# A fused SSM-convolution and gated-MLP kernel with its gradients: tables built earlier, four step buffers, spectral sets at named places, and the last phase's loads moved

## The chip, the cores and the metric

The kernel runs on one core of one Trainium2 chip. The metric is device microseconds of one execution; before the change the median of three runs is 498.83 us (498.76 to 499.54). All times in the views of the profile are microseconds from the start of one profiled execution unless they are marked ns. PE is TensorE's matmul stream, PEld its weight loads, DVE VectorE, ACT ScalarE, POOL GpSimd, SP the queue from which nearly all DMAs are issued.

## The reference

With S = 2048 rows, D = 512 and F = 1376, everything in bf16:

```python
xn = layernorm(x)                         # x = A_q, no weights
k_shift = sum over t of shift_k[:, t] * k shifted by t rows      # 4 taps
kv = k_shift * v
y  = causal convolution along S of kv with ssm_k (length S), by FFT of length 2S
y  = y + kv * ssm_D
out = x + xn * y + ((xn @ w_gate) * (xn @ w_up)) @ w_down
```

The kernel returns out and the gradients, for a given grad_out, of x, k, v, shift_k, ssm_k, ssm_D, w_gate, w_up and w_down: ten arrays.

## The kernel before

All work is bound to one order per engine; the framework places the helpers' instructions by priorities and inserts the waits. There are three kinds of work.

**The MLP by chunks.** `main` runs over eight chunks of 256 rows (NCH). `ffn1(ch)` goes through the eleven blocks of F in six pairs; a pair is 16 matmuls for gate and up (pgu, one PSUM tile of the three-buffer pool P2), 8 for grad_out times w_down (pdh, the two-buffer pool P1), two ACT copies (gu, dh) and two DVE products into hd, which is stored to HDD. `yb(ch)` does the second half of a chunk: for each 128 rows 11 matmuls py (out) and 22 px (dx), with the result bx stored to BX. yb of a chunk runs inside the ffn1 of the next; those of the last two chunks stand at the end, after the marker "wa", which frees the weights and starts the loads goC and xnC.

**The side work.** A generator `side` is stepped beside the chunks, as often as `pace` says: first 170/71 steps per yield of `main`, then GPACE = 0.96. It consists of `front` (normalize the rows, shift k, form the three signals dy, kv and the convolution's kernel; a matmul with the table W1 makes the first step of the Fourier transform, pf, which ACT or DVE copies into fst and SP stores to FD) and of `groups` (eight groups of frequencies: load X from FD, a second transform step ps by table EF, the products in frequency on DVE, the inverse step pg by table EI, stored to GD). `kernel_spec` in `front` transposes ssm_k (ssk) by PE into kn; `wgu_transposes` makes the transposed weights that px needs.

**The last phase.** `dw` forms the weight gradients block by block: `hid_t` transposes a block's hidden values (loaded as hb from HDD) into nath and natd, then 16 matmuls pd and 64 pu. Beside it, at set steps (`every(generator, first step, stride)`), run `inv_y` (loads g from GD, last inverse step pq, products with v and k, stores), `load_kh`, `dsk_gram` (pk), `inv_dk` (po) and `ew` (`final`: out and dx, with bb loaded from BX; `bwd`: dk).

The tables W1, IW, EF and EI are made by the class `Tables`: POOL writes iotas, DVE forms integer phases and folds them by a bitwise and, ACT takes the sine. While the first chunk runs, `tables(n)` is called after pair n and `mid(n)` inside pair n (transposes of w_down by PE, copied to WdT). The first chunk's PE, ACT and DVE order is that of the source (`manual_schedule`) until `first.close()`.

Lines that the text names: L303 the row statistics, L124 and L160 the phase rows, L73 the folds, L76 the sines, L224 and L221 the helpers dve and act (all copies; tell them by their tiles), L347 pf, L493 and L499 pgu and pdh, L527 and L534 py and px, L561 ps, L590 pg, L851 the transposes of hid_t, L873 pq, L957 pd, L973 pu, L799 the load of hb, L793 that of g, L1038 that of bb.

Of the kernel before, what the change touches and what calls it, by code (L numbers as in the profile page):

```python
# [33 lines left out]
class Tables:  # L34
# [43 lines left out]
    def small_phases(self):  # L78
        nc = self.nc
        tmp = self.tmp  # L80
        self.tiw = tmp.tile([P, 2, P], I32, name="tiw")
        for c, off in enumerate((128, 256)):
            nc.vector.tensor_scalar(self.tiw[:, c, :], self.odd[:], self.pf[:, 0:1], float(off + 256), op0=ALU.mult, op1=ALU.add)
        self.fold(self.tiw, 512)
        kk = self.col("kk")
        nc.vector.tensor_scalar(kk[:], self.pf[:], 2.0, 1.0, op0=ALU.mult, op1=ALU.add)
        self.tiv = tmp.tile([P, 2, P], I32, name="tiv")
        for c, off in enumerate((128, 256)):
            nc.vector.tensor_scalar(self.tiv[:, c, :], self.lin[:], kk[:, 0:1], float(off + 256), op0=ALU.mult, op1=ALU.add)
        self.fold(self.tiv, 512)  # L90

    def small_sins(self):
        self.W1 = self.tab.tile([P, 2, P], BF, name="W1")
        self.IW = self.tab.tile([P, 2, P], BF, name="IW")
        self.iwf = self.tmp.tile([P, 2, P], F32, name="iwf")
        self.sin(self.W1[:], self.tiw, 512)
        self.sin(self.iwf[:], self.tiv, 512)
# [41 lines left out]
    def inverse_phases(self):  # L139

        nc = self.nc
        tmp = self.tmp
# [3 lines left out]
        b = self.col("gb")  # L146
        nc.vector.tensor_scalar(b[:], q4[:], 8.0, 1.0, op0=ALU.mult, op1=ALU.add)
        nc.vector.scalar_tensor_tensor(b[:], k2[:], 2.0, b[:], op0=ALU.mult, op1=ALU.add)
        t = self.col("gt")
        nc.vector.tensor_scalar(t[:], j[:], 512.0, None, op0=ALU.mult)  # L150
        nc.vector.tensor_tensor(b[:], b[:], t[:], op=ALU.add)
        pa = tmp.tile([P, 16, 16], F32, name="pa")
        nc.vector.tensor_tensor(pa[:], self.patR[:], self.patG[:].unsqueeze(2).to_broadcast((P, 16, 16)), op=ALU.mult)
        pb = tmp.tile([P, 16, 16], F32, name="pb")
        nc.vector.scalar_tensor_tensor(pb[:], self.patR[:], b[:, 0:1], pa[:], op0=ALU.mult, op1=ALU.add)
        self.tii = ti = tmp.tile([P, 16, 2, 2, 16], I32, name="tii")
        for yi in range(2):
            for c in range(2):
                off = ((2048, 0), (4096, 2048))[yi][c]
                nc.vector.tensor_scalar(ti[:, :, yi, c, :], pb[:], float(off + 4096), None, op0=ALU.add)  # L160
        self.fold(ti, 8192)
# [15 lines left out]
def kernel(  # L177
# [70 lines left out]
    Drow = const.tile([1, D], BF, name="Drow")  # L248
    skb = const.tile([P, 4, D], BF, name="skb")
    mv = const.tile([P, R, 2], F32, name="mv")  # L250
    std = const.tile([P, R], F32, name="std")
# [7 lines left out]
    ybo = wy_es.enter_context(tc.tile_pool(name="ybo", bufs=2, side="right"))  # L259
    wa_es = ExitStack()  # L260
# [12 lines left out]
    for t in hds:  # L273
        nc.gpsimd.memset(t[96:128, NFB - 1], 0.0)

    tab_es = ExitStack()
    TB = Tables(nc, const, wY, tab_es.enter_context(tc.tile_pool(name="tabt", bufs=1, side="right")))

    XG = {}

    def load_x(b):
        x = stp.tile([P, 2, D], BF, name="x_b")
        nc.sync.dma_start(x[:], x_n[:, 2 * b:2 * b + 2, :])
        go = stp.tile([P, 2, D], BF, name="go_b", bufs=3)
        nc.sync.dma_start(go[:], go_n[:, 2 * b:2 * b + 2, :])
        XG[b] = (x, go)
# [11 lines left out]
    def norm_stats(b, root=True):  # L298
        x, go = XG[b]
        stats = stp.tile([P, 2, 6], F32, name="stats")  # L300
# [7 lines left out]
    def norm_std(b):  # L308
        rb = slice(2 * b, 2 * b + 2)
        nc.scalar.activation(std[:, rb], mv[:, rb, 1], ACTF.Sqrt, bias=eps_t[:, 0:1], scale=1.0)  # L310

    def norm_rows(b):
        x, go = XG[b]
        rb = slice(2 * b, 2 * b + 2)
        xn = stp.tile([P, 2, D], BF, name="xn_b", bufs=3)
        nc.vector.reciprocal(rstd[:, rb], std[:, rb])
# [22 lines left out]
    def stage1(sig, src, i, r, evac):  # L339

        if r % 2 == 0:
            FST[sig] = stp.tile([P, 2, 2, D], BF, name="fst")
# [12 lines left out]
    def pre(b):  # L355
# [21 lines left out]
        kv = ST["st1"].tile([P, 2, D], BF, name="kv_b")  # L377
# [8 lines left out]
    def kernel_spec():  # L386
        def tr(r0):
# [6 lines left out]
            act(kn[:], pt[:])  # L394
# [83 lines left out]
    def ffn1(ch):  # L478
# [3 lines left out]
        for fb0 in range(0, NFB, 2):  # L482
# [21 lines left out]
            if ch == 0:  # L504
                mid(fb0 // 2)
# [3 lines left out]
            act(dh[:fw, :n], pdh[:fw, :n])  # L509
            with tc.high_priority(offset=SOON):  # L510
# [5 lines left out]
            yield  # L516

    def yb(ch):
        hd = HD.pop(ch)
        bx = ybo.tile([P, 2, 2, D], BF, name="bx")  # L520
        xb = ybo.tile([P, 2, D], BF, name="xb", bufs=1)
        nc.sync.dma_start(xb[:], x_n[:, 2 * ch:2 * ch + 2, :])
        for sb in range(2):
# [6 lines left out]
            yield  # L530
            px = P1("px", [P, D])
            for t, W in ((1, WTS[0][:, 0]), (2, WTS[0][:, 1])):
                for fb, (f0, fw) in enumerate(FBLK):
                    nc.tensor.matmul(px[:], lhsT=hd[:fw, fb, t, ss], rhs=W[:fw, fb, :], start=(t == 1 and fb == 0), stop=(t == 2 and fb == NFB - 1))  # L534
            act(bx[:, sb, 1, :], px[:])
            if sb == 1:
                nc.sync.dma_start(BX[:, 2 * ch:2 * ch + 2, :, :], bx[:])
            yield
# [84 lines left out]
    load_x(1)  # L623
    load_w(nc.sync, *WPARTS[2])
    nc.sync.dma_start(ssk[:], A_ssm_k.rearrange("(c p) s -> p c s", p=128))
# [6 lines left out]
    warm(ident, 36)  # L632
    norm_stats(0)
# [5 lines left out]
    TB.small_phases()  # L639
    norm_stats(1, False)  # L640
# [8 lines left out]
    def mid(n):  # L649

        if n == 0:
            wd_transposes(*WPARTS[1])
        elif n == 2:
            wd_transposes(*WPARTS[2])

    def tables(n):

        if n == 0:
            norm_std(1)
            norm_rows(1)  # L660
            TB.small_sins()
            TB.forward_base()
        elif n == 1:
            TB.forward_phases()
        elif n == 2:
            TB.forward_sin()
            TB.inverse_phases()
        elif n == 3:
            TB.small_scale()
            TB.forward()  # L670
            TB.inverse_sin()
        elif n == 4:
            TB.inverse()
# [36 lines left out]
    def groups():  # L710
# [5 lines left out]
        pace[0] = GPACE  # L716
        for _ in range(4):
            yield
# [8 lines left out]
        yield  # L727
        yield
# [14 lines left out]
    GPACE = 0.96  # L743
# [4 lines left out]
    def main():  # L748
        for ch in range(NCH):
            it = ffn1(ch)  # L750
            for n, _ in enumerate(it):
                if ch == 0:
                    tables(n)
                yield
                if n == 1 and 0 < ch < NCH - 1:
                    load_xt(ch + 1)
                if ch == 0 and n == 3:
                    load_xt(1)
                if n == (5 if ch == 1 else 1) and 0 < ch < NCH - 1:
                    while len(WTS) < 2:  # L760
                        next(side)
                    yield from yb(ch - 1)
        yield "wa"
        yield from yb(NCH - 2)
        yield from yb(NCH - 1)

    mainit = main()
    acc = -5 * pace[0]
    mdone = 0
    for tag in mainit:  # L770
        if tag == "wa":
            wa_es.close()
            c1 = ctx.enter_context(tc.tile_pool(name="c1", bufs=1, reuse_waits="tile"))
            xnC = c1.tile([P, R, D], BF, name="xnC")
            goC = c1.tile([P, R, D], BF, name="goC")
            nc.sync.dma_start(goC[:], go_n)
            nc.sync.dma_start(xnC[:], XN[:])
        acc += pace[0]
        while acc >= 1:
            acc -= 1  # L780
            next(side, None)
    for _ in side:
        pass
    gpool["es"].close()


    c1n = ctx.enter_context(tc.tile_pool(name="c1n", bufs=1, reuse_waits="tile"))
    c1b = ctx.enter_context(tc.tile_pool(name="c1b", bufs=2, reuse_waits="tile"))
    nats = {}

    def load_g1(sg, r0):
        t = c1b.tile([P, 2, 4, D], BF, name="g1")
# [3 lines left out]
    def load_hb(fb):  # L796
        f0, fw = FBLK[fb]
        t = c1b.tile([P, NCH - 1, 3, 256], BF, name="hb")
# [3 lines left out]
    hbs = {}  # L802
    TURNED = range(NFB - 3, NFB)

    def load_t(fb):

        f0, fw = FBLK[fb]
        if fw < P:
            t = c1n.tile([P, NCH - 1, 3, 2, fw], BF, name="natT", tag="natd", bufs=2)
        else:  # L810
            t = c1b.tile([P, NCH - 1, 3, 2, fw], BF, name="natT", tag="hb")
# [4 lines left out]
    def last_t(fb):  # L816
# [5 lines left out]
        n7 = c1n.tile([P, 3, 2, P], BF, name="nat7", tag="nath")  # L822
# [15 lines left out]
    def hid_t(fb, t):  # L838
# [4 lines left out]
        if t == 0:  # L843
            nats[fb, 0] = c1n.tile([P, R, P], BF, name="nath")
        elif t == 1:
            nats[fb, 1] = c1n.tile([P, 2, R, P], BF, name="natd", bufs=2)
# [7 lines left out]
    load_hb(0)  # L854
    pend = [load_g1(0, 0), load_g1(1, 0)]
    load_hb(1)
# [25 lines left out]

    def inv_y():
        gq = pend
        todo = [(sg, r0) for r0 in range(0, R, 4) for sg in (0, 1)][2:]
        for r4 in range(0, R, 4):
# [8 lines left out]
            for i in range(0, 4, 2):  # L895
# [4 lines left out]
                nc.vector.tensor_tensor(dks[:, r0:r0 + 2, :], dd[:], vb[:], op=ALU.mult)  # L900
                nc.vector.tensor_tensor(kb[:], dd[:], kb[:], op=ALU.mult)
# [9 lines left out]
    def load_gk(dh, rh):  # L911
        t = c1b.tile([P, 2, 8, 256], BF, name="gk", tag="g1")
# [34 lines left out]
    def dw():  # L947
        og = None
        for t in range(3):
            hid_t(0, t)  # L950
            yield
# [118 lines left out]
    def load_kh():  # L1070
        khC = c2.tile([P, R + 3, D], BF, name="khC", tag="o5k")
        nc.gpsimd.memset(khC[0:1, 0:3, :], 0.0)
        nc.sync.dma_start(khC[:, 3:3 + R, :], k_n)
        nc.sync.dma_start(khC[1:113, 0:3, :], k_n[0:112, R - 3:R, :])
        nc.sync.dma_start(khC[113:128, 0:3, :], k_n[112:127, R - 3:R, :])
# [13 lines left out]
    def ew():  # L1089
        load_fin(0)  # L1090
# [10 lines left out]
    sides = [every(seq(inv_y(), load_kh(), load_dk()), 0, 3), every(dsk_gram(), 30, 2), every(inv_dk(), 38, 3), every(ew(), 10, 3)]  # L1101
# [38 lines left out]
```

## Time and profile before

| | us |
|---|---|
| median of 3 runs | 498.83 |
| profiled execution | 499.7 |
| its span, first to last instruction | 497.9 |
| PE busy | 473.3 (95%) |
| DVE busy | 341.1 (68%) |
| ACT busy | 316.3 (64%) |
| POOL busy | 6.7 (1%) |
| mean granted TensorE clock | 0.992 |
| DMA moved | 140.40 MB, mean 282 GB/s |

The shares are means over stages with different limits. The stages by time: the first chunk and the tables to about 35, the front beside chunks 1 and 2 to about 125, the groups beside chunks 3 to 7 to about 312, the last y and dx to 325.7, the last phase to the end. In a row of an order of time the first number is the start, the second the duration, and the bracket gives the idle time of that engine before the row and what ended it. In the list of waits the numbers are total us, times, longest.

### The profile page before, as it was taken

How to read it: one execution, taken by the hardware profiler on the slowest of the kernel's cores; microseconds unless marked ns; L12 is line 12 of the kernel's file. 1: busy time of each engine (PE TensorE's matmuls, PEld its weight loads, DVE VectorE, ACT ScalarE, POOL GpSimd, SP SyncE). 2: the span in 40 equal slices, each digit the busy share in tenths (PEclk: the TensorE clock that was granted, in tenths of full speed). 3: DMA queues.
4: the chain of work that ended last, by engine and by line, in shares of the span. 5: the costliest groups of instructions: out<-in, count | busy, mean ns of one | idle time of the engine just before them, and what ended most of it. 6: DMA issues, size and time to landing. Idle time of an engine off the chain costs nothing.

```text
span 497.9 us, 10465 instructions
## 1 busy us (share of the span) xinstructions
PE 473.3 (95%) x4294; PEld 316.6 (64%) x4331; DVE 341.1 (68%) x633; ACT 316.3 (64%) x352; POOL 6.7 (1%) x17
## 2 busy tenths in 40 slices
PE   7799979999899999999999999999999999999996
PEld 7586654646646636646546753458676887787775
DVE  3987998899347565865946787112258997999760
ACT  3667678865865957959849994377664635363241
POOL 3000000000000000000000000020000000000000
PEclk9998999999999999999999999999999999999999
DMA  9999997999897876968957668799999999999933
GB/s 274 376 316 330 285 311 224 346 305 337 281 304 254 214 252 201 261 234 278 267 170 240 212 209 319 271 373 371 374 388 298 346 383 340 293 286 271 256 118 109
DMA packets 112524, 140.40 MB, mean 282 GB/s; under 512 B 33306, under 2 KB 86879, under 8 KB 110940
## 3 DMA queue, kind: packets, MB, share of 16 engines
q1 hardware_dynamic: 111148, 138.94, 86.3%
q10 hardware_dynamic: 1328, 0.79, 0.5%
q8 instruction: 34, 0.56, 0.5%
q14 instruction: 14, 0.11, 0.1%
HBM read 68.97 MB, written 63.41 MB: 266 GB/s over the span
## 4 chain that ended last, share of the span: by engine, by line
PE 69%; DMA 10%; DVE 9%; ACT 7%; issue 3%; SPq 1%; ACTq 0%; DVEq 0%
PE px L534 15%; PE pgu L493 13%; PE pu L973 10%; PE py L527 7%; PE pdh L499 6%; PE pd L957 5%; PE pf L347 3%; PE pg L590 3%; PE ps L561 2%; PE pt L851 2%; DMA out_dram<-o 2%; DMA bb<-BX 2%; DMA x_b<-in_A_q_dram 2%; ACT gu L221 2%; PE po L928 1%
## 5 line engine op out<-in xcount | busy, mean ns | idle before, releaser
L534 PE MATMUL px<-WT,hd 128*128 128x512 bf16 (+1 forms) x346 | 78.9, 380 | 0.5 <-issue 0.3
L973 PEld LDWEIGHTS <-xnC 128*128 128x128 bf16 x704 | 67.2, 98 | 8.1 <-issue 0.3
L534 PEld LDWEIGHTS <-hd 128*128 128x128 bf16 (+1 forms) x352 | 33.5, 98 | 42.7 <-issue 3.7
L973 PE MATMUL pu<-natd,xnC 128*128 128x256 bf16 x512 | 58.8, 273 | 0.2 <-ACT nath L221 0.2
L493 PE MATMUL pgu<-xt,Wu 128*128 128x256 bf16 (+1 forms) x352 | 54.4, 278 | 3.5 <-DVE WdT L224 2.0
L221 ACT CAST gu<-pgu 128x1024 bf16<-128x1024 f32 (+1 forms) x48 | 45.3, 945 | 15.1 <-PE pgu L493 14.8
L493 PE MATMUL pgu<-xt,Wg 128*128 128x256 bf16 (+1 forms) x352 | 53.8, 276 | 0.0
L221 ACT CAST GO<-pg 128x1024 bf16<-128x1024 f32 x48 | 46.3, 1019 | 7.7 <-issue 4.8
L577 DVE TENSOR_TENSOR T<-SP 128x2048 bf16<-128x2048 bf16 x24 | 29.4, 1224 | 31.9 <-ACT SP L221 31.9
L499 PE MATMUL pdh<-gt,WdT 128*128 128x256 bf16 (+1 forms) x352 | 47.2, 275 | 1.7 <-DVE WdT L224 1.6
L221 ACT CAST SP<-ps 128x1024 bf16<-128x1024 f32 x48 | 46.6, 1033 | 1.9 <-PE ps L561 1.9
L221 ACT CAST fst<-pf 128x1024 bf16<-128x1024 f32 x40 | 39.2, 1032 | 11.2 <-DMA FD<-fst 6.1
L493 PEld LDWEIGHTS <-Wu 128*128 128x128 bf16 (+1 forms) x352 | 33.3, 101 | 20.2 <-issue 15.1
L527 PE MATMUL py<-Wd,hd 128*128 128x512 bf16 (+1 forms) x166 | 40.5, 380 | 0.8 <-issue 0.5
L221 ACT COPY natd<-pt 128x2048 bf16<-128x2048 bf16 x16 | 30.1, 1880 | 17.7 <-PE pt L851 17.7
L499 PEld LDWEIGHTS <-WdT 128*128 128x128 bf16 (+1 forms) x352 | 35.1, 101 | 7.0 <-DVE WdT L224 1.9
L221 ACT CAST bx<-px 128x512 bf16<-128x512 f32 x16 | 9.5, 592 | 46.1 <-PE px L534 46.1
L493 PEld LDWEIGHTS <-Wg 128*128 128x128 bf16 (+1 forms) x352 | 35.4, 102 | 4.2
L511 DVE TENSOR_TENSOR hd<-gu 128x512 bf16<-128x512 bf16 (+1 forms) x48 | 19.1, 398 | 26.3 <-ACT gu L221 26.3
L221 ACT CAST og<-pu 128x1024 bf16<-128x1024 f32 (+1 forms) x11 | 10.9, 993 | 33.9 <-PE pu L973 24.1
L512 DVE TENSOR_TENSOR hd<-gu,dh 128x1024 bf16<-128x1024 bf16 (+1 forms) x48 | 30.8, 643 | 1.8 <-ACT dh L221 0.9
L527 PEld LDWEIGHTS <-hd 128*128 128x128 bf16 (+1 forms) x176 | 16.3, 98 | 22.8 <-issue 4.8
(164 smaller groups left out, 708.0 us busy)
## 6 DMA issues: line engine op xcount, KB each, us to landing
HDD<-hd SPq DMA_DIRECT2D x35, 384.0 KB, 4.5
FD<-fst SPq DMA_DIRECT2D x24, 512.0 KB, 3.9
X<-FD SPq DMA_DIRECT2D x24, 512.0 KB, 5.0
GD<-GO SPq DMA_DIRECT2D x24, 512.0 KB, 3.8
hb<-HDD SPq DMA_DIRECT2D x8, 1344.0 KB, 10.0
g<-GD SPq DMA_DIRECT2D x8, 1024.0 KB, 8.9
BX<-bx SPq DMA_DIRECT2D x8, 512.0 KB, 3.5
bb<-BX SPq DMA_DIRECT2D x8, 512.0 KB, 8.4
```

Source lines behind the costliest of these rows:

```text
L221: nc.scalar.copy(o, i)
L347: nc.tensor.matmul(pf[:, c, :], lhsT=TB.W1[:, c, :], rhs=src[:, i, :], start=True, stop=not point)
L493: nc.tensor.matmul(pgu[:w, i, t, :], lhsT=W[:, c, f0:f0 + w], rhs=xt[:, :, c, :], start=(c == 0), stop=(c == NC4 - 1))
L499: nc.tensor.matmul(pdh[:w, i, :], lhsT=WdT[:, c, f0:f0 + w], rhs=gt[:, :, c, :], start=(c == 0), stop=(c == NC4 - 1))
L511: nc.vector.tensor_tensor(hd[:fw, fb0:fb0 + n, 0, :], gu[:fw, :n, 0, :], gu[:fw, :n, 1, :], op=ALU.mult)
L512: nc.vector.tensor_tensor(hd[:fw, fb0:fb0 + n, 1:3, :], gu[:fw, :n], dh[:fw, :n].unsqueeze(2).to_broadcast((fw, n, 2, 256)), op=ALU.mult)
L527: nc.tensor.matmul(py[:], lhsT=hd[:fw, fb, 0, ss], rhs=Wd[:fw, fb, :], start=(fb == 0), stop=(fb == NFB - 1))
L534: nc.tensor.matmul(px[:], lhsT=hd[:fw, fb, t, ss], rhs=W[:fw, fb, :], start=(t == 1 and fb == 0), stop=(t == 2 and fb == NFB - 1))
L577: tt(W[:].rearrange("p c a d -> p c (a d)"), A[:, i:i + 1].rearrange("p c a d -> p c (a d)").to_broadcast((P, 2, 2 * D)), B[:].rearrange(" ...
L590: nc.tensor.matmul(pg[q // 2][64 * a:64 * a + 64, q % 2, :], lhsT=TB.EI[32 * q:32 * q + 32, 2 * g + a, yi].rearrange("p k c -> p (k c)"), ...
L957: nc.tensor.matmul(pd[:fw, :], lhsT=nat_h(fb, r), rhs=goC[:, r, :], start=(r == 0), stop=(r == R - 1))
L973: nc.tensor.matmul(pu[:, c, :, :fw], lhsT=xnC[:, r, cs(c)], rhs=nat_d(fb, r), start=(r == 0), stop=(r == R - 1))
```

## The change

- **Tables.** Each table's steps are split. forward_base moves ahead of the first x's statistics, W1's phases and sine and the forward phases stand right after the first xt, inverse_base and inverse_phases go from DVE to POOL (DVE keeps three small column steps and the fold, now inverse_fold), and the rest is dealt anew to pairs 0 to 3. The statistics of the second x move from ahead of the first pair to pair 1, the second xt to pair 3, and the manual order ends one pair earlier. The memsets of the two hd tiles move behind POOL's iotas, and the second go's load behind the last weights'. The w_down transposes of part 2 stand behind the ACT copies of pair 2.
- **Buffers.** x_b has four buffers and is normalized in place (xn_b is gone), kv overwrites v, rstd takes std's place, fst has four buffers, stats one. ACT's copy of kn gets high priority.
- **Sets.** Once the groups begin, `pace` is None and `side` is stepped once at each true yield: after every second pair in chunks up to 4 and after every pair but the last in later ones, after py, at the new yield "half" in the middle of px, and after px. The first steps of `groups` are spaced anew, and the side work begins two yields earlier (-3 instead of -5).
- **Last phase.** The helpers of the last phase move ahead of `main`. `open_c` finishes the groups, opens the pools and issues the loads of hb 0, two g and hb 1 before the last yb, and the three hid_t of block 0 run inside that yb. The BX store of the last chunk goes from SP's queue to ACT's. The loads of k and of the first bb are issued under `issue_after` with a named DVE product (rows 10 and 2), dks and kb products get high priority, and the other generators start three steps earlier, as `dw` has three steps fewer.

```diff
+    def inverse_base(self):
+        e = self.nc.gpsimd
...
+        e.tensor_scalar(b[:], q4[:], 8.0, 1.0, op0=ALU.mult, op1=ALU.add)
+        e.tensor_tensor(b[:], b[:], k2[:], op=ALU.add)
+        e.tensor_tensor(b[:], b[:], k2[:], op=ALU.add)
...
     def inverse_phases(self):
+        e = nc.gpsimd
-        nc.vector.tensor_tensor(pa[:], self.patR[:], self.patG[:]...)
+        e.tensor_tensor(pa[:], self.patR[:], self.patG[:]...)
-        nc.vector.scalar_tensor_tensor(pb[:], self.patR[:], b[:, 0:1], pa[:], op0=ALU.mult, op1=ALU.add)
+        e.tensor_scalar(pb[:], self.patR[:], self.gb[:, 0:1], None, op0=ALU.mult)
+        e.tensor_tensor(pb[:], pb[:], pa[:], op=ALU.add)
...
-                nc.vector.tensor_scalar(ti[:, :, yi, c, :], pb[:], float(off + 4096), None, op0=ALU.add)
-        self.fold(ti, 8192)
+                e.tensor_scalar(ti[:, :, yi, c, :], pb[:], float(off + 4096), None, op0=ALU.add)
+    def inverse_fold(self):
+        self.fold(self.tii, 8192)
...
-        x = stp.tile([P, 2, D], BF, name="x_b")
+        x = stp.tile([P, 2, D], BF, name="x_b", bufs=4)
...
-        xn = stp.tile([P, 2, D], BF, name="xn_b", bufs=3)
+        xn = x
...
-            FST[sig] = stp.tile([P, 2, 2, D], BF, name="fst")
+            FST[sig] = stp.tile([P, 2, 2, D], BF, name="fst", bufs=4)
...
-        kv = ST["st1"].tile([P, 2, D], BF, name="kv_b")
+        kv = v
...
-            act(kn[:], pt[:])
+            with tc.high_priority(offset=SOON):
+                act(kn[:], pt[:])
...
-            yield
+            yield n > 1 and (ch > 4 or fb0 % 4 == 0)      # ffn1
...
+                if t == 1:
+                    yield "half"                          # yb, inside px
...
-                nc.sync.dma_start(BX[:, 2 * ch:2 * ch + 2, :, :], bx[:])
+                (nc.scalar if ch == NCH - 1 else nc.sync).dma_start(BX[:, 2 * ch:2 * ch + 2, :, :], bx[:])
...
+    TB.forward_base()
     norm_stats(0)
...
-    TB.small_phases()
-    norm_stats(1, False)
+    TB.small_phases_w()
+    TB.small_sin_w()
+    TB.forward_phases()
+    TB.inverse_base()
+    TB.inverse_phases()
...
     def tables(n):
         if n == 0:
+            TB.forward_sin()
+            TB.small_phases_v()
+            TB.inverse_fold()
+        elif n == 1:
+            TB.inverse_sin()
+            TB.small_sin_v()
+            norm_stats(1, False)
         elif n == 2:
             norm_std(1)
             norm_rows(1)
+            TB.forward()
         elif n == 3:
+            load_xt(1)
+            TB.inverse()
             TB.small_scale()
...
-        pace[0] = GPACE
-        for _ in range(4):
-            yield
+        pace[0] = None
+        yield
...
+    def open_c():
+        for _ in side:
+            pass
+        gpool["es"].close()
...
+        load_hb(0)
+        pend.extend((load_g1(0, 0), load_g1(1, 0)))
+        load_hb(1)
...
-        yield from yb(NCH - 1)
+        open_c()
+        for n, tag in enumerate(yb(NCH - 1)):
+            yield tag
+            if 1 < n < 5:
+                hid_t(0, n - 2)
...
+        if pace[0] is None:
+            if tag and tag != "wa":
+                next(side, None)
+            continue
...
+        with tc.issue_after(DKS[10].ins):
+            nc.sync.dma_start(khC[:, 3:3 + R, :], k_n)
...
+        with tc.issue_after(DKS[2].ins):
+            load_fin(0)
```

## The prediction

> **What bounds the kernel now.** I read the page first, for the share of each engine.
>
> ```profile
> PE 473.3 (95%) x4294; PEld 316.6 (64%) x4331; DVE 341.1 (68%) x633; ACT 316.3 (64%) x352; POOL 6.7 (1%) x17
> ...
> PE   7799979999899999999999999999999999999996
> ...
> PEclk9998999999999999999999999999999999999999
> ```
>
> PE is busy for 473.3 of 497.9 us, and the changed program issues the same 8664 PE rows in another order. So only PE's idle time, 497.9 - 473.3 = 24.6 us, and slow clock can be won. The table of stretches of 5 us and, around the worst, of 2 us says where they lie.
>
> ```profile
> 14.00:16.00 2.00, 0.38 (x5) 0.25 (x4) 1.97 (x5) 1.38 (x2) 0.00 (x0) 1.00 1.08 318
> ...
> 20.00:22.00 2.00, 0.48 (x9) 0.37 (x7) 1.97 (x5) 1.49 (x2) 0.00 (x0) 1.00 1.03 412
> 22.00:24.00 2.00, 1.56 (x9) 1.12 (x9) 1.65 (x6) 2.00 (x3) 0.00 (x0) 0.65 1.02 394
> 24.00:26.00 2.00, 2.00 (x11) 1.45 (x10) 1.79 (x12) 0.05 (x2) 0.00 (x0) 0.50 1.05 386
> ...
> 66.00:68.00 2.00, 0.33 (x2) 0.19 (x2) 1.63 (x3) 1.01 (x1) 0.00 (x0) 1.00 1.04 364
> ```
>
> The columns are PE, PEld, DVE, ACT and POOL busy, then clock, DMA share and GB/s. PE loses 1.62 us at 14, 1.96 us at 20.4 to 22.4, and then runs at 0.65 and 0.50 of its clock: (1 - 0.65) x 2 + (1 - 0.50) x 2 = 1.7 us more. The same happens at 38 to 44 (clock 0.92, 0.50, 0.73: again 1.7 us). Before 2.17 and after 493.5 PE has no work at all (6.6 us), which the change leaves alone. What ended PE's waits:
>
> ```profile
> PE pf L347 <- ACT fst L221: 3.7, 4, 2.0
> ...
> PE pf L347 <- ACT kn L221: 2.0, 2, 1.1
> PE pgu L493 <- DVE WdT L224: 2.0, 1, 2.0
> PE pdh L499 <- DVE WdT L224: 1.6, 1, 1.6
> PE ps L561 <- ACT GO L221: 1.5, 4, 0.7
> ```
>
> The chain of waits agrees: 69% of it is PE. From 130 to 300 (the groups) the stretches leave PE idle 3.2 us in all, from 330 to 490 1.9 us. Everything below is therefore PE's waits, one stage after another.
>
> **The change, part by part.**
>
> *First 30 us.* These are the rows behind the first two waits:
>
> ```profile
> 12.86 0.69 DVE L303 BATCH_NORM_STATS2 stats<-x_b 128x6 f32<-128x512 bf16 x1 [2.35 <-DMA x_b<-in_A_q_dram]
> ...
> 14.48 1.19 DVE L224 COPY WdT<-pw 128x2048 bf16<-128x2048 bf16 x1
> ...
> 19.96 1.00 DVE L124 TENSOR_SCALAR ti<-patF,fr,fbase 128x512 int32<-128x512 f32 x2
> ...
> 20.99 0.69 DVE L73 TENSOR_SCALAR ti<-ti 128x1024 int32<-128x1024 int32 x1
> ...
> 21.60 0.78 DVE L224 COPY WdT<-pw 128x1216 bf16<-128x1216 bf16 x1
> ...
> 22.44 0.89 PE L493 MATMUL pgu<-xt,Wu 128*128 128x256 bf16 x4 [1.96 <-DVE WdT L224]
> ```
>
> The first WdT copy stood behind the statistics of the second x, which waited for their DMA; pw was done at 12.4. Now DVE does the forward phases there: from 8.8 the three tiw rows (0.47 + 0.29), two ti rows (1.00), the fold (0.69) and six column rows (0.8) end near 12.1. WdT runs 12.4 to 13.6, PE reaches its pdh at 14.1, and the 1.62 us are gone. forward_base (14 rows, 17.37 to 19.10: 1.7 us) moves ahead of the first x, which lands at 4.6; DVE idles there (3.75 us), so it is free.
>
> The second wait: PE, 1.62 us earlier, has its transposes done at 18.9 and then needs ACT's gu copy of pair 2. ACT now has the inverse sine (1.06 us) and iwf (0.40) ahead of that copy; the sine waits for DVE's fold of tii (0.69), and the fold for POOL, which takes over 2.4 us of DVE rows (four column steps 0.61, pa 0.42, pb 0.48, tii 0.90). DVE reaches the fold at 13.6 + hd 1.05 + tiv 1.1 = 15.7; 15.7 + 0.69 + 1.06 + 0.40 + gu 1.02 = 18.9, just in time. So every us that POOL is later than 15.7 is a us of PE, and queued behind the fold on DVE are hd of pair 1, the statistics of x 1 and the next WdT copy. POOL arithmetic is in no row. POOL's narrowest rows take 0.1 to 0.2 us: five chained column steps after gk (12.1) end near 13.4. Then six 256-wide steps: from below DVE's own rows (0.23 to 0.48, 1.8 us in all), from above POOL's memset of 1536 elements (1.37 us) for each, 8.2 us. The nearest row is POOL's iota 128x256, 0.41 us: 2.5 us, and with 0.1 us between them tii stands at 16.5, 0.8 us late. Bounds: 0 and 6 us. Value: 1.96 - 0.8 = 1.2 us won, and the 1.7 us of clock with it (bounds 0 and 1.7).
>
> The Trainium skill ("GPSIMD Engine Reference", section 3, Performance versus the Vector engine) puts a two-input elementwise step on this engine at about twice the Vector engine's time and a one-input one near line rate; an estimate from DVE's rows by it would have tii at about 15.8, and the sum 0.7 us better. No row shows it here.
>
> New waits behind that: the order has 13 transposes of ssk before the second xt. ssk (2 MB) is the eighth large load; by the bandwidth row 7.4 MB are moved at about 23 us, when PE arrives (cost 0 to 2.6 us, taken 0.6). The step back to Sqrt costs ACT a table load (1.28 us) ahead of gu of pair 3, hidden by the transposes. kn stands behind gu of pair 4 on ACT, which costs PE 1.5 us where it now waits 1.12 + 0.25; the second kn stands behind the skb copy (1.23 us), itself behind skt's DMA (5 us): about 1.3 us. Against these stands the second slow stretch of clock, which may or may not come: 0.8 of its 1.7. Sum: 1.6 + 1.2 + 1.7 + 0.3 (an xt wait) - 0.6 - 0.1 - 1.3 + 0.8 = **3.6 won**, bounds 5.5 won and 2 lost.
>
> *30 to 75.* ACT and DVE waited for FD stores to free fst (ACT 6.1 us in 5, DVE 0.4), and the one of them that reached PE is the gap at 65.7 to 67.7 (2.02 us, then 0.25). Four fst buffers take it away. The priority of kn may take part of the 0.86 and 0.66 us that PE waits for kn; I take none for sure. **2.0 won**, bounds 0.5 and 3.5.
>
> *75 to 130.* x and kv now overwrite their sources, so the v loads wait on SP for PE's kv matmuls; behind them queue FD and KS stores. One front step (8 to 9 us) passes before v is needed, a v load lands in 3.2 to 5.1. PE idles 2.6 us here, of which some 0.5 goes since DVE has 2.4 us less to do; the first group comes one pair (2.6 us) earlier after the last kv store, and its X load (5.0 us) may cost 0.5. **Nothing**, bounds 1.5 and -2.
>
> *Groups.* A pair takes PE 2.6 us and ACT 1.6; a set adds 0.7 to PE and 2.05 to ACT. With a set at every pair, ACT needs 3.65 against 3.3. Sets now stand at every second pair and after each half of px (2.4 us) in chunks 3 and 4, but still at every pair in 5 to 7. Of 3.2 us I take **1.0**, bounds 0 and 2.
>
> *Last y and dx.* hid_t of block 0 now stands after 4 of the last py matmuls:
>
> ```profile
> 316.36 0.46 SPq L799 DMA_DIRECT2D hb<-HDD  x1
> ```
>
> ```profile
> DMA to landing us min/median/max: 7.5/9.6/11.7
> ```
>
> The first is the queue's row in order of time, the second is from the view of the tile hb, whose first load, needed at 325.5, can only be the one of 7.5. Now hb's issue stands behind the BX store of chunk 6, which waits for ACT's last bx: 1.1 us after the last yb starts. PE gets there after py 2.4 + px 4.8 + 0.9 = 8.0. Landing after 7.5 costs 0.6 us, after 9.6 2.7 us. What it replaces was about 0.5 us (waits on nath and pt). **1.2 lost**, bounds 0.5 won and 3.6 lost. The BX store on ACT's queue (0.46 us) meets an idle ACT.
>
> *Last phase.* bb's wait (DVE, 10.4 us) goes, but PE had its work meanwhile: nothing. The 2 MB of k and two bb (1 MB) now stand on SP before the first kb stores, the dks copies and the fourth g. **Nothing**, bounds 0.3 and -2.7.
>
> Sum: 3.6 + 2.0 + 0 + 1.0 - 1.2 - 0 = 5.4. The profiled execution took 499.7 (span 497.9 and 1.8 around it): 494.3. The median of before is 498.83, 0.9 below it, so I forecast **493.4**.
>
> **The rivals.** *DVE is the front's bound.* From 40 to 125 it is busy 77.4 of 85 us; then PE's early gain comes back as waits for hd, fst and kv, and only the 2.4 us taken from DVE stay, with the groups' 1.0, less 1.2: 2.2 won, 496.6. For it: five stretches of 4.96 and more. Against: these rows are partly ks work that nothing waits for at once, and DVE too starts earlier. 0.20.
>
> *POOL's table is late.* The place is the fold on DVE. The whole gain is gone when tii stands 0.8 + 5.4 = 6.2 us late, at 21.9, that is at (21.9 - 13.4) / 6 = 1.4 us for each wide step, the memset row. With 1.7 us each it is 7.9 us late and the time 493.4 + 7.1 = 500.5. Against: the iota row is 3.4 times shorter. 0.06. The Trainium skill ("SBUF — State Buffer", Who interferes with whom) has GpSimd and a DVE step with two SBUF inputs, or in a two-port mode, shut each other out of a shared port for a whole instruction, which would push the same way; no row here has both at work.
>
> *The last phase waits for loads.* k and bb put 3.1 MB, at 0.38 MB per us 8.2 us, ahead of the fourth g, whose issue at 341.95 landed just when PE wanted it (0.4 us of wait at 350.9). If they are still in flight when it is issued, about 12 us after the first pq, PE waits up to 8.2 us: 500.4 with 7.0 of it. Against: between the start of the last yb and then, 34 us x 0.38 = 12.9 MB can move, and 12.5 MB are asked (three hb of 1.38, three g and two BX 3.7, v and k rows 1.0, bb 1.05, k 2.1, the rest small). It decides when the DMA engines run below 0.36. 0.09. That k's load isn't held back by its pin belongs here: in the built queue it stands before the kb stores of the first rows.
>
> *No change*: ssk (2.0 more) and hb (2.4 more) at their bounds, with nothing from the groups (1.0), eat the gain: 498.8. 0.05.
>
> **How the numbers follow.** My forecast holds 0.60. A measurement of this kernel can tell 0.2%, 1 us. Faster: 0.60 + 0.20 = 0.80; same 0.05; slower 0.06 + 0.09 = 0.15. The range takes in DVE as the bound, no change, and most of the good bounds (first stage 1.9 better, kernel spectrum 1.5, groups 1.0, transition 0.5): 488.5 to 499.3.
>
> **What would show it.** Right: PE's wait for WdT at 14 and 20 gone and its fourth pair starting by 20.5 at full clock; no fst wait of 2 us; pf's wait for kn still there; a wait of 1 to 3 us on hb at the last py; PE's busy time as before. Wrong: a gap on PE at 19 with DVE's fold waiting for POOL; DVE at 5.0 in all stretches to 125 with PE idle beside it; PE waiting on g about 25 us into the last phase.

## The result, and the profile after

The changed kernel took 496.76 us (median of 21 runs, 493.8 to 502.5) against 499.54 for the kernel before beside it (21 runs): 0.9943 of before, 95% interval 0.9927 to 0.9959, some 2.9 us. The run of 502.5 us counts as slow and is left out of the ratio. A second series gave 0.9933 (0.9909 to 0.9957). The forecast was 493.4, 5.4 us won: the direction held, the size was about twice too large. The profiled execution took 496.1 us, its span 494.2.

From the page, the engines and the slices of PE and of its clock:

```profile
PE 472.5 (96%) x4331; PEld 314.4 (64%) x4331; DVE 339.8 (69%) x623; ACT 317.4 (64%) x352; POOL 13.8 (3%) x29
...
PE   7789999999999999999999999999998989999986
...
PEclk9899999999999999999999999999999999999999
```

PE is idle 494.2 - 472.5 = 21.7 us, 2.9 less than before. The middle is full now; two slices after 370 and one near 475 are not, which were full before. The stretches shown of before (same columns):

```profile
14.00:16.00 2.00, 2.00 (x21) 1.80 (x19) 1.77 (x5) 1.50 (x2) 1.91 (x2) 1.00 1.05 337
20.00:22.00 2.00, 0.04 (x1) 0.04 (x1) 1.93 (x5) 2.00 (x4) 0.00 (x0) 0.88 1.01 403
22.00:24.00 2.00, 2.00 (x10) 1.39 (x10) 1.77 (x4) 1.98 (x3) 0.00 (x0) 0.50 1.03 394
24.00:26.00 2.00, 2.00 (x16) 1.58 (x14) 0.85 (x4) 1.66 (x3) 0.00 (x0) 0.76 1.05 388
66.00:68.00 2.00, 2.00 (x27) 1.49 (x25) 0.64 (x2) 2.00 (x3) 0.00 (x0) 1.00 0.84 250
```

The gaps at 14 and 66 are gone. The one at 20 is not: it grew, and the slow clock behind it is there again. What ended PE's waits:

```profile
PE pgu L513 <- ACT gu L235: 3.3, 1, 3.3
PE pq L907 <- DMA g<-GD: 1.9, 3, 1.4
PE pk L1033 <- DMA khC<-in_A_k_dram: 1.9, 1, 1.9
PE pf L366 <- ACT kn L235: 1.6, 1, 1.6
...
PE ptd L979 <- DVE dDs L976: 1.3, 1, 1.3
```

Before, fst (3.7), WdT (3.6) and kn (2.0) led this list. Now a copy of gu leads it, and three waits of the last phase (g, khC, ptd) stand high in it. The sums of this view by stage, in us (waits put down to "issue" are left out, PE's wait at its start belongs to the first stage, the wait for the first X to the groups):

| stage | before | changed | changed, second profile |
|---|---|---|---|
| 0 to 40 | 7.5 | 8.3 | 6.6 |
| 40 to 75 | 3.8 | 0.4 | 0.7 |
| 75 to 135 | 2.2 | 0.9 | 0.8 |
| groups, to 295 | 2.0 | 0.9 | 1.5 |
| 295 to 330 | 0.2 | 0.6 | 0.6 |
| from 330 on | 1.0 | 5.3 | 5.1 |

The middle got better and the last phase worse. The last pgu tells the same. It ends at 291.0 before and at 284.5 and 285.2 after, 6.5 and 5.8 us earlier. From there to its end PE takes 202.5 us before and 205.3 and 205.1 after, although 32 matmuls of the groups now stand ahead of that point (some 1.3 us, an estimate from their 0.04 us of busy time each).

### The profile page after: what moved, and what is told of

Its sections match the earlier page's. It is cut to its first block, busy times and chain, and to the rows that moved or that the text cites. A ratio compares the mean times of both kernels' runs of the same rounds, so it can differ in the third digit from the quotient of the medians.

```text
span 494.2 us, 10487 instructions
## 1 busy us (share of the span) xinstructions
PE 472.5 (96%) x4331; PEld 314.4 (64%) x4331; DVE 339.8 (69%) x623; ACT 317.4 (64%) x352; POOL 13.8 (3%) x29
## 4 chain that ended last, share of the span: by engine, by line
PE 60%; DMA 15%; DVE 13%; ACT 4%; SPq 3%; issue 2%; POOL 1%; ACTq 0%; DVEq 0%
PE pgu L513 12%; PE px L556 12%; PE pu L1007 8%; PE pdh L519 5%; DMA g<-GD 5%; PE py L549 5%; PE pd L991 4%; PE pt L834 3%; PE pg L614 3%; DMA x_b<-in_A_q_dram 2%; PE ps L585 2%; PE pf L366 2%; DMA out_dram<-dk 2%; PE pq L907 2%; PE pk L1033 2%
## 5 line engine op out<-in xcount | busy, mean ns | idle before, releaser
L556 PE MATMUL px<-WT,hd 128*128 128x512 bf16 (+1 forms) x352 | 81.0, 380 | 0.0
L235 ACT CAST og<-pu 128x1024 bf16<-128x1024 f32 (+1 forms) x11 | 10.9, 993 | 39.4 <-PE pu L1007 25.5
L601 DVE TENSOR_TENSOR U<-SP 128x2048 bf16<-128x2048 bf16 x24 | 29.2, 1218 | 0.0
```

The source lines that it names most:

```text
L235: nc.scalar.copy(o, i)
L601: tt(W[:].rearrange("p c a d -> p c (a d)"), A[:, i:i + 1].rearrange("p c a d -> p c (a d)").to_broadcast((P, 2, 2 * D)), B[:].rearrange(" ...
```

## The experiments

Each ratio is to the kernel before, on the same chip, with its 95% interval. A thousandth is half a us.

**The changed kernel again.** No edit.

> The changed kernel once more, unedited, beside the next three on the same chip. In the first study the median of the granted clock over its runs was 0.992 with 496.8 us, that of before on the next chip 0.997 with 500.4. Theory (the gain is there at full clock, time x clock 493.1 against 498.7, 5.6 us, and about 2 us of it are given back in slow stretches of clock that come in some runs after a gap of PE of 2 us or more, of which the changed kernel still has one of 3.3 at 22 and others of 1.9 and 1.4 in the last phase): again 0.993 to 0.996 of before, a mean clock 0.003 to 0.005 below that of before, and a second profile in which the slow stretch after 22 us may be there or not. Rival (the two chips differ, the clock has no part): the same clock as before within 0.001.

0.9933 (0.9909 to 0.9957). The mean granted clock of its runs was 0.9939, of before beside it 0.9959; in the first series it was 0.9924. Time x clock, run by run and averaged, gives 493.7 against 498.3: by this the change wins about 4.6 us at full clock, and 1.0 of them goes to the clock. That is an upper bound for the clock. Over 258 runs on record, compared within one kernel on one chip, a us of slow clock, (1 - clock) x span, goes with only 0.51 us of time (standard error 0.07). One reason is in the traces: a part of a slow stretch often falls into a gap of PE or behind PE's end. So the clock takes 0.5 to 1.0 us here. The theory's direction holds, its size (2 us) doesn't. The prediction counted on the opposite, because the profile of before shows two slow stretches (mean clock 0.992): of the 94 runs of before that the comparisons below count 83 had a higher clock, and the median is 0.996 to 0.997.

**The front: the fold later.**

```
 tables(0): TB.forward_sin(); TB.small_phases_v()
-           TB.inverse_fold()
 tables(1):
-           TB.inverse_sin()
            TB.small_sin_v(); norm_stats(1, False)
+           TB.inverse_fold()
 tables(2):
+           TB.inverse_sin()
            norm_std(1); ...
```

> The changed kernel with one edit: the fold of tii on DVE stands behind the statistics of the second x, and the inverse sine on ACT ahead of the square root of that x, one pair of blocks later each; the work on POOL stays as it is. Theory (the mis-sized term is POOL: tii stands at 18.9 where the prediction had 16.5, and the queue of DVE waits 3.1 us for it with hd of pair 1 behind): the wait of PE for gu at 22 (3.3 us) goes to under 0.6, the clock stays at 1.0 from 20 to 25 (1.7 us), and the time falls by 3 to 5 us to about 492.5, 0.985 of before. Rival (DVE or ACT bounds the front to 75, so that what PE wins early it waits for later): the wait moves to hd, xt or kn before 45 us and the time falls by less than 1 us, 0.992 or more of before.

First the changed kernel's own rows, in order of time:

```profile
12.94 0.94 POOL L166 TENSOR_SCALAR pb<-patR,gb 128x256 f32<-128x256 f32 x1
13.96 1.19 POOL L167 TENSOR_TENSOR pb<-pb,pa 128x256 f32<-128x256 f32 x1
15.24 3.64 POOL L172 TENSOR_SCALAR tii<-pb 128x256 int32<-128x256 f32 x4
...
18.92 0.69 DVE L73 TENSOR_SCALAR tii<-tii 128x1024 int32<-128x1024 int32 x1 [3.08 <-POOL tii L172]
19.65 1.06 ACT L76 ACTIVATE zi<-tii 128x1024 bf16<-128x1024 int32 x1 [3.99 <-DVE tii L73]
...
20.92 0.99 ACT L235 CAST gu<-pgu 128x1024 bf16<-128x1024 f32 x1
21.96 1.01 PE L513 MATMUL pgu<-xt,Wu 128*128 128x256 bf16 x4 [3.26 <-ACT gu L235]
```

POOL, DVE, ACT, PE: the chain that the prediction named, 3.26 us long at PE. The edit takes it away, and in its profile this stands in its place:

```profile
25.43 1.21 PE L411 MATMUL ptk<-ident,ssk 128*128 128x128 bf16 x16 [3.04 <-DMA ssk<-in_A_ssm_k_dram]
```

0.9951 (0.9927 to 0.9974): no gain, the rival's time but not the waits that it named. ssk is issued at 11.4 in both kernels and lands 14.1 us later, at 25.5. The wait for POOL covered the wait for ssk.

**The table back on DVE.** `e = nc.vector`, both helpers between the fold of tiv and that of tii.

> The changed kernel with the steps of the inverse table on DVE again, between the fold of tiv and that of tii, in the place that they now have in the order. Theory (POOL needs 7.4 us, 11.5 to 18.9, for what takes DVE 2.4; on DVE the fold starts at about 18.3, as late as now, so the move to POOL is worth nothing here): PE waits 2.5 to 3.5 us for gu as now, the time within 1 us of the changed kernel, 0.992 to 0.996. Rival (the 2.4 us taken from DVE come out at PE, as the rival of the prediction that has DVE as the bound says): 2 to 3 us above it, 0.998 to 1.000.

0.9933 (0.9908 to 0.9957), PE's wait for gu 3.3 us as with POOL. The theory holds: the move to POOL is worth nothing that shows. That speaks against the prediction's rival that DVE bounds the front, though the measured time is near that rival's 496.6: 2.4 us of DVE work put back cost nothing.

**The front: the side work later too.** `acc = -4 * pace[0]` on top of the later fold.

> The kernel of the later fold, and also the first step of the side work one place later (start at -4 in place of -3), so that PE has the fifth pair of blocks ahead of the transposes of ssk. Theory (two waits lie one behind the other at 19 to 25: the table of POOL, and behind it ssk, which lands at 25.4; taking away the first alone gave nothing, 0.995): no gap of PE over 1 us between 15 and 30, no slow stretch of clock there, 0.986 to 0.990 of before. Rival (then DVE bounds the front, and PE waits for kn, fst, dy or hd later): PE idles 4 us and more between 30 and 130, 0.993 and above.

0.9959 (0.9935 to 0.9983). No gap is left from 15 to 30, and PE stands 3.5 us at 40, for kn. The rows behind that:

```profile
29.70 0.48 SPq L703 DMA_DIRECT2D skt<-in_A_shift_k_dram  x1
...
36.98 1.23 DVE L705 COPY skb<-skt 128x2048 bf16<-128x2048 bf16 x1 [3.27 <-DMA skt<-in_A_shift_k_dram]
...
38.29 1.86 ACT L235 COPY kn<-ptk 128x2048 bf16<-128x2048 bf16 x1 [4.32 <-DVE skb L705]
```

skt sits in one of kn's two buffers. Its load takes 7.3 us, and the copy of kn waits until skb is out of it: a third wait behind POOL and ssk.

**skt in a buffer of its own**, alone and with the shifted front (both with k behind the last g, below). `skt = stp.tile([P, D, 4], BF, name="skt", tag="fst", bufs=4)`.

> The kernel with k behind the last g, and skt in a step buffer (fst) in place of one of the two of kn. Theory (POOL at 22 is the bound that counts as long as it stands, so a wait behind it that is taken away gives little): PE still waits 3.3 us for gu at 22, the wait for kn near 32 (1.6) may shrink, within 1 us of the kernel with k alone. Rival (the buffer of kn is what paces the whole stretch from 30 to 45, whatever happened ahead of it): 2 us or more below it.

> That kernel with the later fold and the side work one place later, as in the shifted front. Theory (POOL, ssk and skt stand one behind the other, and only without all three is the front faster): no gap of PE over 1.5 us between 15 and 75, no slow stretch of clock there, 2.5 to 5 us below the kernel with k alone, 0.975 to 0.981 of before. Rival (a fourth bound, the DMA engines, whose share is 1.0 from 5 to 45 us, or DVE): the gap moves once more to fst, dy or v between 40 and 110, and the time is within 1 us of the kernel with k alone or above it.

0.9996 (0.9975 to 1.0016) and 0.9964 (0.9939 to 0.9989), both above the kernel with k alone (0.9904). With skt in a step buffer PE waits 5.0 us for DVE's fst in the second, and for dy_b (2.5) and fst (1.9) in the first. Four waits (POOL's table, ssk, skt, fst) lie one behind the other, and in these edits each took the place of the one removed. That the step buffer lent to skt cost more than kn's second one gave is how the times read; no run separates the two. What the front would be worth without all of them is not shown.

**Two step buffers again.** `name="fst", bufs=4` to `name="fst"`.

> The changed kernel with two step buffers in place of four (the size before). Theory (the buffers give more than the 2.0 us of the sum, since the idle time of PE from 40 to 75 fell from 4.2 to 0.9 us, with a slow stretch of clock of 1.5 us): the waits of pf on fst come back with 3 us of idle PE between 40 and 75, and the time rises by 3 to 4 us, to about 1.000 of before. Rival (the gap went because of the new order in the front, and the buffers would not be needed): within 1 us of the changed kernel, 0.993 to 0.996.

1.0011 (0.9988 to 1.0035), 3.4 us above the first series of the changed kernel and 3.9 above the second. The waits are back, spread out:

```profile
PE pf L366 <- ACT fst L235: 1.8, 3, 0.8
...
PE pgu L513 <- ACT fst L235: 0.7, 2, 0.4
PE pf L366 <- DVE fst L238: 0.7, 3, 0.3
```

More of PE's idle time came between 75 and 130 (0.9 to 3.8 us) than between 40 and 75 (0.9 to 1.4). The theory holds in its size, not in its place. The buffers are worth as much as the whole net gain.

**The sets on a pace.** `pace[0] = 0.96` and the first steps of `groups` spaced as before.

> The changed kernel with the sets of the groups on a pace again (0.96 of a set at each place, four places before the first set), as before. Theory (the named places are worth the 2.7 us that the idle time of PE fell between 135 and 295): PE idles some 2.5 to 3 us there and the time rises by about 2.5 us, to 0.999 of before. Rival (the priority of the copies and the four x buffers took those waits and the places do nothing; the sum had 1.0 us): idle time there below 1 us and the time within 1 us of the changed kernel.

1.0037 (1.0015 to 1.0059), but not through the sets: the edit also moved k's load behind every g, and

```profile
411.69 3.63 PE L1034 MATMUL pk<-khC,dks 128*64 128x256 bf16 x32 [6.29 <-DMA khC<-in_A_k_dram]
```

with slow clock from 408.6 to 415.4, across the end of this wait. Inconclusive for the sets, so they were run again with k in one place (next but one).

**k's load: the pieces early, then the whole of it held.** The pins name DKS[10] and DKS[2], which are DVE products; the loads are on SP. Built without both pins the program is the same, instruction by instruction: these pins do nothing. A pin on an instruction of SP itself holds, as the runs below show. SP's rows of the changed kernel:

```profile
326.71 1.51 SPq L1072 DMA_DIRECT2D bb<-BX  x2
328.27 0.97 SPq L1108 DMA_DIRECT2D khC<-in_A_k_dram  x1
336.77 1.54 SPq L939 DMA_DIRECT2D out_dram<-kb  x2
...
340.11 0.92 SPq L775 DMA_DIRECT2D g<-GD  x1
...
399.38 0.51 SPq L1109 DMA_DIRECT2D khC<-in_A_k_dram  x1
```

The 2 MB go out at 328, where the pin would have them after row pair 10 (the store of its kb is issued at 377), the fourth g behind them at 340, and the two small pieces that pk needs as much 71 us later. PE's rows show which of these loads it waited for:

```profile
347.61 1.89 PE L907 MATMUL pq<-g,IW 128*128 128x512 bf16 x8
...
376.07 1.90 PE L907 MATMUL pq<-g,IW 128*128 128x512 bf16 x8 [1.35 <-DMA g<-GD]
...
407.18 1.94 PE L1033 MATMUL pk<-khC,dks 128*64 128x256 bf16 x32 [1.85 <-DMA khC<-in_A_k_dram]
```

These are the fourth pq, the seventh, and the first pk. The fourth g landed at 347.3, just in time; PE waited for the seventh and for k's pieces. In the second profile of the changed kernel the same three stand at 348.2 (no wait), 376.7 (1.7 us) and 408.7 (2.0 us, put down to DVE's tk, which pk does not read; a piece of k landed at 408.2). Two edits:

```
-        with tc.issue_after(DKS[10].ins):
+        with tc.high_priority(offset=SOON):                                  # pieces early
+        with tc.high_priority(offset=SOON), tc.issue_after(KST[6].ins):      # held: KST is SP's own kb store
             nc.sync.dma_start(khC...)   # three
```

> The changed kernel where the load of k in the last phase has priority in place of its pin: the large transfer stays at about 328 us, and its two small pieces are issued near 372 in place of 399. Theory (the last phase lost time through the two pieces, which stand on the queue of SP behind 50 other issues): the wait of pk at 407 (1.9 us) goes and the time falls by 1.5 to 2 us, to 0.990 of before. Rival (PE is held there by something else that is late too, or the wait moves to kd, gk or dDs): the idle time of PE from 400 on stays, and the time is within 0.7 us of the changed kernel.

0.9908 (0.9874 to 0.9942), 1.7 us below the first series of the changed kernel and 1.2 below the second, which a comparison of this length can't tell from nothing. The profile is clearer: pk's wait is gone, and from the end of the last px to its own end PE takes 167.4 us in place of 169.3 and 169.1. That is the theory's size. PE waits 3.3 us for g instead of 1.9.

> The changed kernel where the load of k is really held: all three pieces are issued behind the store of row pair 8 on the queue of SP (near 372), with priority. Theory (the 2 MB of k at 328 to 340 take bandwidth from g and from v and k rows, and so the last phase loses): the waits of PE for g fall from 1.9 to under 0.7 us, that of pk for khC is gone, 0.988 of before. Rival (g waits since its issue stands on the queue of SP behind stores that wait for DVE, whatever k does): g waits 2 to 3.3 us, the last of them longest since 2 MB of k go just ahead of it, and the time is that of the kernel with the early pieces, 0.991, or above.

0.9871 (0.9846 to 0.9897), beside the changed kernel's 0.9933: 3.1 us, the lowest ratio of all kernels here. Of PE's waits for g one is left:

```profile
324.90 0.60 SPq L775 DMA_DIRECT2D g<-GD  x1
325.55 1.54 SPq L1073 DMA_DIRECT2D bb<-BX  x2
331.62 0.53 SPq L775 DMA_DIRECT2D g<-GD  x1
...
385.52 1.90 PE L907 MATMUL pq<-g,IW 128*128 128x512 bf16 x7 [2.25 <-DMA g<-GD]
```

The fourth g goes out 8.5 us earlier than with k ahead of it, and the wait that stays is for the last one, which is issued at 375.3 with k's 2 MB just ahead (the longest landing of a g is 10.2 us, the median 7.9). From the end of the last px to its own end PE takes 167.3 us, the time of the early pieces, where the 2 MB still go out at 328. So the profiles give the pieces some 1.9 us and show nothing for holding the 2 MB; the other 1.2 of the 3.1 us lie ahead of 320, where k has no part yet, or in the spread of the runs. PE's waits for g came to 2.3 us, against 1.9 and 2.7 in the changed kernel, so the theory's under 0.7 was missed. The rival is right that a load placed ahead of a g delays that g, and wrong on the time.

**The sets again**, with k's priority as in the early pieces; in this order all three are issued between 371 and 379. Against the kernel just shown.

> The kernel with the groups' sets on a pace, and the load of k with priority, so that its three pieces are issued together near 372 as in the kernel where k is held; against that kernel only the places of the sets differ. (The first run of the paced sets lost 6.3 us to a late k, and so says little of the sets.) Theory (the named places are worth 1.6 us, the idle time of PE between 135 and 295 that came back in the first run of the paced sets): 1 to 2.5 us above the kernel where k is held. Rival (nothing, or the whole 2.7 us and more): within 0.7 us, or 3 us and more above it.

0.9887 (0.9866 to 0.9908), 0.8 us above it. The two intervals overlap: the named places may be worth nothing or up to 2.5 us, and hardly 3. From 135 to 295 PE waits 0.0 us with the places and 1.9 with the pace.

**k right behind the last g.** `issue_after` with the last g load, which is SP's own.

> The changed kernel with one edit: the three pieces of the load of k are issued right behind the last g on the queue of SP. Theory (early k costs the last phase its waits for g and khC, 3.9 us in the profile of the changed kernel, and by a slow stretch of clock now and then): no wait for g or khC over 0.5 us, and 0.983 to 0.987 of before. Rival (holding k back gains only by chance of one profile): 0.990 or above.

0.9904 (0.9870 to 0.9938). No wait for g or khC is left, yet it isn't faster than k held: kd, ptd and hb hold PE 5.5 us after 390. Expectation missed: other waits, on DVE's products and on hb, took the place of those removed, and from the last px on PE takes 170.1 us.

**The last y and dx as before.** `open_c()` behind the loop, the three `hid_t` at the head of `dw`, the starts three later. With k's priority, without it, and with k behind the last g:

> The last y and dx as before (the first loads of the last phase behind them, the transposes of block 0 as the first steps of dw), the rest as changed, with the load of k given priority (near 385, all three pieces). The prediction had 1.2 us lost by the changed place, since the first hb would land late; the trace shows hb issued at 304.7 and no wait for it. Theory (the changed place costs nothing and saves the 0.5 us of waits on nath and pt): idle time of PE from 295 to 330 0.6 to 1.2 us in place of 0.6, 0.990 to 0.992 of before. Rival (the early loads crowd the start of the last phase, so the old place is better): 0.988 or below.

1.0043 (1.0026 to 1.0061): k had got ahead of the last g, PE waited 6.2 us for it, and slow clock came twice, across the end of this wait (3.4 us) and behind a later gap of 2.2 us (1.7). It says nothing of the place.

> The changed kernel with the last y and dx as before (the first loads of the last phase behind them, the transposes of block 0 as first steps of dw), k left as the scheduler then places it (late, behind the last g), since in the first try the priority put 2 MB of k ahead of the last g (6.2 us of wait), which says nothing of the place. Theory (the changed place costs PE nothing and saves some 0.3 us, the prediction's 1.2 us lost was wrong): PE idles 0.6 to 1.0 us from 295 to 330, and with the last phase in the order of before the time is 0.990 to 0.995 of before. Rival (the place was worth much, 3 us or more, since the loads of the last phase start 12 us earlier with it): waits for g or hb of 3 us and more, 0.999 or above.

> The kernel before in this list (k behind the last g) with the last y and dx as before the change. Theory (the changed place costs PE nothing and saves 0.3 us of waits on nath): 0 to 1 us above the kernel before in this list, PE idle 0.6 to 1.0 us from 295 to 330. Rival of the prediction (the changed place costs 1.2 us, since hb lands late): 1 to 2 us below it.

0.9911 (0.9887 to 0.9935), in spite of 4.5 us of wait for khC: 1.6 us below the first series of the changed kernel and 1.1 below the second (errors of about 1.4 and 1.7 us). And 0.9883 (0.9855 to 0.9910), 1.0 us below its partner (error 2.2). The new place is not shown to win anything, and may cost 1 to 1.6 us.

**All together**: shifted front, k behind the last g, priority for dDs.

> All that the studies point to: the front of the run with the shift, the load of k behind the last g on the queue of SP with all three pieces together, and priority for the copy of dDs. Theory (the gains add, since they lie in different stages: k held gave 3.1 us with 2.3 us of wait for the last g left, ptd waited 1.2, the front 2 to 4): 0.976 to 0.981 of before, a mean clock of 0.997 or more. Rival (they do not add, since the chain of DVE bounds the last phase and the front): 0.985 or above.

0.9969 (0.9947 to 0.9990): the gains don't add. Against the shifted front alone (0.9959) PE's idle time from 330 to 420 falls from 5.9 to 1.7 us in the profile, but behind 420 it rises from 0.2 to 4.0: ptd, which the priority did not help, waits 2.2 us for dDs, and po 1.3 for kd. So most of that wait moved. The version to take is the changed kernel with k held on SP's own store, though four others, from 0.988 to 0.991, aren't clearly apart from it.

## Why the prediction was right and wrong

Up to the last pgu the sum had 6.6 us won (3.6 + 2.0 + 0 + 1.0). The two profiles of the changed kernel show 7.8 and 7.1: PE is there 6.5 and 5.8 us earlier, with 1.3 us more of the groups done. Behind it the sum had 1.2 lost, and 4.1 and 3.9 were. So the step that failed is the last phase, put at nothing. That the first part came out near its forecast is luck: the front brought about 1 us in place of 3.6, and the stretch from 40 to 135 some 4.6 in place of 2.0. The second step that failed is the clock terms: the profile of before, from which they come, had about one slow stretch more than most runs of before.

- *Last phase, nothing, bounds 0.3 and -2.7.* PE's waits from 330 on rose from 1.0 to 5.3 and 5.1 us: for the seventh and eighth g (1.7 and 2.7), for k's small pieces (1.9 and 2.0), and for dDs (1.3 and 0.2). The pieces are shown as a cause: both edits that bring them forward take the wait away and 1.9 us of the phase with it. The rest stays open: with k behind the last g no wait for g or k is left, and kd, ptd and hb hold PE as long. The rival that named this stage (500.4, 0.09) had the pin right, and the place wrong: it had PE wait up to 8.2 us for the fourth g, which landed in time (0.5 us of wait with the early pieces). The prediction had seen in the built queue that k stood before the first kb stores, and priced it at nothing; the two small pieces, 71 us behind, it did not name.
- *Front, 3.6 won, 1.7 and 0.8 of it clock.* In the first 40 us PE's waits went from 7.5 to 8.3 and 6.6, and the slow clock that began there from 3.4 (two stretches) to 1.7 and 3.4. The first wait (pdh, 1.6 us) went as worked out. The second did not, and so its clock came again. The chain through the fold was right, and the sign named for it came, but the row was not right: 0.41 us for a wide step stood in, 0.91 to 1.19 were measured behind gk, and tii came at 18.9 in place of 16.5, within the bounds given. By the prediction's own rule that costs 3.2 us instead of 0.8, and PE did wait 3.3. But taking POOL's lateness away won nothing: ssk (25.5 in place of "about 23", 3.0 us of wait in place of 0.6) lay right behind.
- *The clock terms* took one profiled execution of before as the rule. Most runs of before have fewer slow stretches, and the changed kernel kept a gap long enough to bring one: 0.5 to 1.0 us lost in the second series in place of 2.5 won. If half a us of time goes with a us of slow clock here too, 2.5 was also too high a price for the two.
- *Four step buffers, 2.0 won*: 3.4 to 3.9, at the upper bound or above, since they also carry the stretch from 75 to 130, put at nothing. *Sets, 1.0 won*: 0.8, not clear of its error.
- *Last y and dx, 1.2 lost.* The cause named, hb landing late, isn't there: hb was issued at 304.65 and PE did not wait for it at the last py. The two runs without the new place lean towards a loss of that size. By what, is open.

## What to carry to other kernels

A wait that ends last hides the one behind it: before a wait is priced, ask when everything else that the waiting instruction and its next ones need has landed. A pin is worth only what the built queue shows: name an instruction of the queue that issues the load, and move all pieces of a load together. One execution's slow clock is a draw, so it belongs in the range and not in the sum. A total that comes out right up to some point proves nothing for its terms; compare stage by stage.

## What the runs showed of the hardware

*Slow clock comes in whole steps, by chance.* In all 18 profiles every slow stretch but the one behind PE's end lasts 3.41 us at half the clock, 1.7 us lost, or twice that. The same gap of 2.9 to 3.3 us at 22 (13 profiles) was followed by one at once in 8 of them (in one by two); in 3 the clock held there and fell behind the next wait, 1.6 us long; in 2 it didn't fall at all. This is one of those three (k held), the stretch at 22 and the ones after 32:

```profile
22.00:24.00 2.00, 2.00 (x20) 1.78 (x20) 1.74 (x4) 1.98 (x3) 0.00 (x0) 1.00 1.02 390
...
32.00:34.00 2.00, 1.75 (x8) 0.80 (x9) 1.20 (x3) 0.66 (x3) 0.00 (x0) 0.89 1.07 360
34.00:36.00 2.00, 2.00 (x19) 1.98 (x18) 0.34 (x1) 1.19 (x2) 0.00 (x0) 0.50 1.06 438
36.00:38.00 2.00, 2.00 (x16) 1.86 (x15) 2.00 (x4) 1.03 (x1) 0.00 (x0) 0.76 1.01 434
```

(1 - 0.89) x 2 + (1 - 0.50) x 2 + (1 - 0.76) x 2 = 1.7 us. Gaps of 4.5 to 6.3 us (four profiles) always brought 3.4. But the clock fell 1.5 to 3.9 us before such a gap ended, so that PE's own work lost 1.5 to 2.7 of them. The Trainium skill ("TensorE: Matmul & The Clock Gate", Part 1) has a free-running window of 3.4 us by which the clock is set, and half the clock after an idle one: 1.7 us a window, and the chance, agree. That a whole window of idle is needed does not: a gap of 1.6 us was enough here at times, and in the profile of before one of 1.1 with one of 0.3 behind it.

*POOL is slow in one-input steps as well.* Four 256-wide f32 to int32 steps took it 3.64 us (the row of tii above), most of it with DVE idle beside them; DVE did them in 0.90 us before. The Trainium skill ("GPSIMD Engine Reference", section 4.1) puts one-input steps near line rate; here the factor is 4.
